# Half-size products for the first layer of a feed-forward network behind an attention: seven instead of eight, two units of tokens at once

## The chip, the cores and the metric

The kernel runs on one core of a Trainium2 chip. The metric is the device time in microseconds from the start to the end of one execution; the median of three runs is given. The core has a matrix engine (TensorE, PE in the profile, with its own queue of weight loads, PEld), VectorE (DVE), ScalarE (ACT), GpSimd (POOL), a queue that issues transfers (SyncE, SP), and 16 DMA engines. Products land in PSUM, which the kernel uses as four double banks of 128 x 2 x 512 floats.

## The reference

Attention over 8 batches, 8 heads, 576 positions and 64 dimensions, with a window of 32 positions for the first four heads and a window of 128 positions with a stride of 4 for the others, and then a feed-forward network over the 4608 x 512 result:

```python
scores = np.where(masks, scale * q @ k.T, -1e9)
attn = exp(scores - max) / (sum + 1e-9)
x = (attn @ v) as 4608 x 512
h = x @ w_in                         # 512 x 2048
sp = np.where(h > 20.0, h, np.log1p(np.exp(np.minimum(h, 20.0))))
g = h * np.tanh(sp)
out = g @ w_out                      # 2048 x 512
```

Inputs and output are float32.

## The kernel before, in words

The tokens are cut into 16 units, half a batch each, of 288 tokens. Per unit there are four pairs of heads; their attention takes small products, and the feed-forward network takes the large ones. Products of float32 accuracy are made from float16 parts: each operand is split into a high and a low part, and three of the four products of parts are added up (low weight by high x, high weight by low x, high by high). The first four units ("direct") compute their attention in float32 on PE; units 4 to 15 use split parts and transposes by DMA.

The first layer (`ff1`, L830 to L844) of a unit takes four chunks of 512 columns of the weights (index j). A call makes two blocks of 128 columns. Each block has 12 matmuls of 128 x 128 weights by 288 tokens: four parts of the 512 inputs times three products of parts. ScalarE then applies Mish to the double bank (L844). A gate (`gate`, L855 to L862) scales the chunk and splits it: high part on ScalarE (L860), low part on VectorE (L862). The second layer (`ff2`) makes again 192 matmuls of the same shape per unit (L872), ScalarE scales the result (L886) and SP stores it (L888). All weights stay in SBUF: `w1`, four tiles of 128 x 4 x 2 x 512, and `w2`.

Ahead of that stand, for units 4 to 15, `prep` (maxima of q, k and v on VectorE, L291, then scales and splits), `scores_of_pair` (L597), `scores` on VectorE (scale and mask L621, maximum L627, subtraction L629), `exps` on ScalarE (L668), `transpose_p` (split L704 and L706, DMA transpose L709), `values` (L745 to L760) and `transpose_x` (split L776 and L778, DMA transpose L781). At the beginning the weights arrive as 64-bit words and are turned into float16 parts (`w_load`, `w_max`, `w_words`, `w_split`; L323 to L396). Matmuls on a tile of zeros (`keep_warm`, L901) fill time on PE at the beginning.

Nothing schedules at run time: the string ORDER lists steps by hand, about 2,000 of them (`ff4.2=0`: unit 4, first half of chunk 1, bank 0; a name that stands again continues the step behind its next `yield`). Each engine executes its instructions in that order, and so does SP with the transfers. Semaphores make an instruction wait for its operands and buffers.

Of the kernel before, what the change touches and what calls it, by code (L numbers as in the profile page):

```python
# [25 lines left out]
SUM_EXP = 14  # L26
TINY = 2.0 ** -40
EXP_BITS = 0x7F800000
P_SCALE = 2.0 ** 14
G_SHIFT = 2.0 ** -14  # L30
# [3 lines left out]
MASKED = -2.0 ** 30  # L34
EPS = 1.0e-9
# [15 lines left out]
tx1.3=0 tx1.3 ww0.2.0 kw10=1 tx1.2=1 tx1.2 sp2.3=2 sc2.3 tx1.3 tx1.3 kw4=0 pr2 pr2 tx1.2 tx1.2 wl1.3.0 wm1.3.0 gt0.0=1
gt0.0 ww1.3.0 wp0.2.0 wp0.2.0 ww1.3.0 wl1.3.1 wm1.3.1 ww1.3.1 ww1.3.1 fs1 kw3=0 ff1.0=0 ff1.0 ff1.0 ff1.1=1 ff1.1
ff1.1 gt1.0=2 ff1.2=3 ff1.2 ff1.2 ff1.3=0 sp2.1=1 sc2.1 ws1.3=3 ws1.3 ff1.3 ex2.3 kw6=2 tp2.3=2 tp2.3 gt0.3 gt1.0
wl1.2.0 wm1.2.0 ww1.2.0 ww1.2.0 wl1.2.1 wm1.2.1 ww1.2.1 ww1.2.1 ex2.1 kw3=3 ff0.2=3 ff0.2 ff0.2 ff0.3=2 ff0.3 ff0.3
gt0.1=3 gt0.1 ff1.6=1 ff1.6 ws1.2=3 ff0.4=2 ff1.6 ws1.2 ff1.3 gt1.1=4 gt1.1 wp1.3.0 wp1.3.0 ff0.4 va2.3=1 ff0.4
tp2.1=0 tp2.1 va2.3 va2.3 wp1.2.1 wp1.2.1 ld3 sp3.0=3 sp3.1=2 lv3 sc3.0 sc3.1 ff1.7=0 ff1.7 ff1.7 gt1.3=5 gt1.3
wp1.2.0 wp1.2.0 wp1.3.1 wp1.3.1 wl1.0.1 wm1.0.1 ff1.4=1 ff1.5=0 ff1.5 ww1.0.1 ff1.4 ff1.4 ff1.5 gt1.2=6 gt1.2 wl1.0.0
wm1.0.0 ww1.0.0 ww1.0.0 va2.1=3 va2.1 va2.1 sp3.3=2 ff0.5=1 ff0.5 ff0.5 gt0.2=7 gt0.2 fo1.2.0=0 fo1.2.1 fo1.2.2
ws1.0=1 ws1.0 ex3.1 tp3.1=3 tp3.1 wl1.1.0 wm1.1.0 fo1.2.3 fo1.2.3 fo1.2.3 sc3.3 ex3.3 sp3.2=3 sc3.2 ex3.2 ww1.1.0
ww1.1.0 sp2.2=1 ld4 sc2.2 pr4 pr4 ex2.2 lv4 fo1.3.0 fo1.3.1 fo1.3.2 fo1.3.3 fo1.3.3 pr3 fo0.2.0=2 fo0.2.1 fo0.2.2  # L60
fo0.2.3 fs2 fo0.2.3 fo0.2.3 pr4 pr4 xa2 tx2.3=3 tx2.3 tx2.3 va2.0=1 tp2.2=0 tp2.2 va2.0 va2.0 wp1.0.0 ex3.0 wp1.0.0
fo0.3.0 fo0.3.1 fo0.3.2 fo0.3.3 fo0.3.3 pr4=0 ww1.0.1 fo1.3.3 pr4 fo0.3.3 tx2.0=3 va2.2=1 tx2.0 va2.2 tx2.0 kw2=2 pr4
# [117 lines left out]
def attn_mish_ffn_kernel(  # L180
# [205 lines left out]
    def w_split(k, g, p):  # L386
# [5 lines left out]
        for v, d, sc in parts:  # L392
            nc.scalar.activation(halves(d, 0), v, AF.Identity, scale=sc)
# [566 lines left out]
```

## Time and profile before

| what | value |
|---|---|
| median of 3 runs | 921.7 us (921.39 to 922.32) |
| the profiled execution, time | 923.0 us |
| the profiled execution, span from first to last instruction | 921.1 us |
| granted TensorE clock | 1.000 |
| moved by DMA | 82.36 MB, mean 89 GB/s |
| read from HBM, written | 49.02 MB, 9.44 MB |
| keep-warm matmuls | 482 |

In the profile's lines, `L841 PE MATMUL b<-x,w 128*128 128x288 f16 x3072` is line, engine and operation; the tile written and the tiles read; the weights' shape and the moving operand's shape and type; and how often. Behind the bar stand busy time in us, the mean duration of one in ns, and the engine's idle time just ahead of these, with what ended it. In a timeline the columns are start, duration and then the instruction with its count, with the idle time before it in brackets.

### The profile page before, as it was taken

Reading aid. Unit: us, or ns where it says so; the run is one execution under the profiler, and the core shown is the slowest. Engines: PE = TensorE matmul, PEld = TensorE weight load, DVE = VectorE, ACT = ScalarE, POOL = GpSimd, SP = SyncE. Lnnn points to the kernel's source line nnn. Section 1 sums busy time; section 2 is a strip of 40 time slices with the busy share of each in tenths; the row PEclk is TensorE's granted clock in tenths of the full one; section 3 lists DMA queues with packets and bytes.
Section 4 is the critical chain, followed back from the end, with each engine's and each line's share of the span. In section 5 each row is a group of like instructions: output and inputs, shape, how many; then the busy total and the mean of one; then the engine's idle time right before and its main releaser. Section 6 shows DMA issues by size and latency. Waiting matters only on the chain.

```text
span 921.1 us, 21816 instructions
## 1 busy us (share of the span) xinstructions
PE 911.5 (99%) x9422; PEld 738.0 (80%) x9422; DVE 593.1 (64%) x879; ACT 545.5 (59%) x804; POOL 22.0 (2%) x99
## 2 busy tenths in 40 slices
PE   9999999999999999999999999999999999999998
PEld 8877878887788877878888888878888888788776
DVE  4877988566867776787967576785546856422020
ACT  3687775673475676756677556776455656644141
POOL 1000000040000000000000000000000000000000
PEclk9999999999999999999999999999999999999999
DMA  9734443130424344424444444326215322212000
GB/s 292 217 117 139 140 139 105 56 105 16 119 81 110 69 106 95 98 62 103 102 100 96 100 72 113 72 55 120 52 33 119 87 55 59 36 41 35 20 14 27
DMA packets 156560, 82.36 MB, mean 89 GB/s; under 512 B 122960, under 2 KB 152368, under 8 KB 156464
## 3 DMA queue, kind: packets, MB, share of 16 engines
q1 hardware_dynamic: 156464, 80.97, 35.5%
q8 instruction: 74, 1.21, 0.5%
q14 instruction: 22, 0.18, 0.1%
HBM read 49.02 MB, written 9.44 MB: 63 GB/s over the span
## 4 chain that ended last, share of the span: by engine, by line
PE 99%; ACT 1%; issue 0%; DVE 0%; ACTq 0%
PE b L872 41%; PE b L841 41%; PE b L597 4%; PE b L745 3%; PE b L901 3%; PE b L739 2%; PE b L716 1%; PE b L594 1%; PE b L649 0%; PE b L352 0%; PE b L349 0%; PE b L800 0%; PE b L787 0%; ACT pp L725 0%; PE b L309 0%; ACT x L802 0%
## 5 line engine op out<-in xcount | busy, mean ns | idle before, releaser
L872 PE MATMUL b<-g,w 128*128 128x288 f16 x3072 | 388.1, 287 | 0.0
L841 PE MATMUL b<-x,w 128*128 128x288 f16 x3072 | 387.3, 286 | 0.0
L841 PEld LDWEIGHTS <-w 128*128 128x128 f16 x3072 | 297.6, 98 | 75.3
L872 PEld LDWEIGHTS <-w 128*128 128x128 f16 x3072 | 297.1, 98 | 75.4
L862 DVE SCALAR_TENSOR_TENSOR g<-hm,sg,g 128x1152 f16<-128x1152 f32 x64 | 89.8, 1414 | 116.8 <-ACT g L860 116.8
L844 ACT ACTIVATE hm<-b,fs 128x576 f32<-128x576 f32 x128 | 92.3, 737 | 102.4 <-PE b L841 88.4
L886 ACT ACTIVATE y<-b,fo 128x288 f32<-128x288 f32 x60 | 43.5, 724 | 126.6 <-PE b L872 116.5
L860 ACT ACTIVATE g<-hm,sg 128x1152 f16<-128x1152 f32 x64 | 79.9, 1253 | 3.2 <-PE b L872 1.6
L668 ACT ACTIVATE sb<-sb,ln_p 96x704 f32<-96x704 f32 (+3 forms) x48 | 42.4, 888 | 26.8 <-DVE sb L629 26.6
L629 DVE TENSOR_TENSOR sb<-sb,nm 72x576 f32<-72x576 f32 (+4 forms) x60 | 45.2, 754 | 2.1
L627 DVE TENSOR_REDUCE nm<-sb 72x8 f32<-72x576 f32 (+4 forms) x60 | 44.9, 748 | 1.7
L760 DVE TENSOR_TENSOR xs<-b,rec 72x512 f32<-72x512 f32 (+1 forms) x64 | 39.7, 620 | 6.5 <-DVE rec L759 0.5
L706 DVE TENSOR_TENSOR p<-sb,p 96x704 f16<-96x704 f32 (+3 forms) x33 | 29.4, 894 | 18.1 <-ACT p L704 18.0
L901 PE MATMUL b<-zeros 128*128 128x128 f16 x482 | 33.4, 229 | 5.1 <-ACT pp L725 2.1
L901 PEld LDWEIGHTS <-zeros 128*128 128x128 f16 x482 | 31.0, 103 | 7.3 <-issue 5.0
L759 DVE RECIPROCAL rec<-den 72x8 f32<-72x8 f32 (+1 forms) x64 | 12.0, 188 | 36.2 <-ACT den L755 27.3
L844 ACT ACT_TABLE_LOAD x22 | 28.2, 1283 | 9.1 <-PE b L841 8.7
L621 DVE SCALAR_TENSOR_TENSOR sb<-b,sc,m_r 96x704 f32<-96x704 f32 (+1 forms) x24 | 23.4, 976 | 15.3 <-PE b L597 6.3
L597 PEld LDWEIGHTS <-q 64*72 64x72 f16 (+1 forms) x1008 | 25.8, 116 | 8.3 <-issue 7.6
L597 PE MATMUL b<-k,q 64*72 64x72 f16 (+3 forms) x1008 | 30.9, 210 | 0.0
L621 DVE SCALAR_TENSOR_TENSOR sb<-b,sc,m_d 72x576 f32<-72x576 f32 (+1 forms) x24 | 22.6, 944 | 11.4 <-PE b L597 11.0
L521 DVE TENSOR_TENSOR q<-qn,q 128x288 f16<-128x288 f32 (+1 forms) x36 | 23.7, 708 | 7.2 <-ACT q L512 7.2
(141 smaller groups left out, 819.0 us busy)
## 6 DMA issues: line engine op xcount, KB each, us to landing
qn<-in_qT SPq DMA_DIRECT2D x16, 576.0 KB
out_T<-y SPq DMA_DIRECT2D x64, 144.0 KB
raw<-in_w_in SPq DMA_DIRECT2D x16, 512.0 KB
raw<-in_w_out SPq DMA_DIRECT2D x16, 512.0 KB
vn<-in_v SPq DMA_DIRECT2D x48, 128.0 KB
knd<-in_kdT SPq DMA_DIRECT2D x16, 208.0 KB
vdn<-in_vd SPq DMA_DIRECT2D x32, 104.0 KB
knp<-in_kT SPq DMA_DIRECT2D x8, 320.0 KB
```

The costliest lines, as they stand in the source:

```text
L597: nc.tensor.matmul(o, q, k, start=start, stop=stop, skip_group_check=True)
L621: nc.vector.scalar_tensor_tensor(args[0], args[1], d["sc"][:nq], args[2], ALU.mult, ALU.add)
L627: nc.vector.tensor_reduce(nm[:nq, :, j:j + n], x, axis=AX.X, op=ALU.max, negate=True)
L629: nc.vector.tensor_tensor(blocked(sb, c0, n, w), x, nm[:nq, :, j:j + n].unsqueeze(3).broadcast_to([nq, 2, n, w]), op=ALU.add)
L668: nc.scalar.activation(x, x, AF.Exp, bias=ln_p[:nq])
L841: nc.tensor.matmul(ph[:, h, :HT], w1[j][:, c, wi, k * P:(k + 1) * P], x_of(d, xi, c), start=(n == 0), stop=(n == len(seq) - 1))
L844: nc.scalar.activation(d["m"][j][:, k0:k0 + 2], ph[:, :, :HT], AF.Mish, scale=d["fs"][:, j:j + 1])
L860: nc.scalar.activation(g[:, 0], m, AF.Identity, scale=sg)
L862: nc.vector.scalar_tensor_tensor(g[:, 1], m, sg, g[:, 0], ALU.mult, ALU.subtract)
L872: nc.tensor.matmul(po[:, :HT], w2[:, e, j, wi, k * P:(k + 1) * P], d["g"][j][:, gi, k, :], start=(j == 0 and n == 0), stop=(j == NCH - 1 a ...
L886: nc.scalar.activation(o, src, AF.Identity, scale=fo)
L901: nc.tensor.matmul(warm[:, 1, 512 - P:], zeros, zeros, start=True, stop=True)
```

## The change

For units 4 to 15 the first layer is made for two units together (a batch, 2 x 288 tokens) by Strassen's scheme in Winograd's form. The 512 inputs are halved (pairs of heads 0 and 1, pairs 2 and 3), each chunk of 512 weight columns is halved, and the tokens are halved into the two units. The eight half-size products of a chunk become seven (`s_p1` to `s_p7`), each with 2 blocks of 128 columns by 6 matmuls of 128x288 (L938). They need four sums of weights and four sums of activations:

- `w_forms` makes the weight sums once, on VectorE (L869 to L881) with a conversion on ScalarE (L879), and stores them and the plain quarters to memory (L887). Since the seven forms don't fit beside the rest, `stream` loads them again for every pair of units: 14 loads of 128 x 2048 float16 (512 KB) into three tiles. These tiles, and buffers for activations, are the places of the old `w1`, which units 4 to 15 no longer read.
- `x_forms` makes the activation sums on VectorE (L908 to L912), splits them (ScalarE L918, VectorE L920) and transposes them by DMA (L923), in place of `transpose_x`.
- Products add up in PSUM, with results taken out in between: bank Y holds product 1, is copied out by ScalarE (L955), then has product 6 added to it, is copied again (L977), has 7 added, is read by VectorE (L983), has 4 added, and goes to Mish. Bank W holds product 5, copied (L962), and then 3, added by VectorE (L997). Product 2 has a bank for itself (added at L969).

In addition: the two units of a pair share one scale (`pf`, from L545); the maxima in `prep` become absolute sums on ScalarE (L511 to L522); for units 4 to 9 (`PE_MASKS`) the mask is added by two matmuls on PE (L646) instead of L621 on VectorE; fewer keep-warm matmuls (303); scales shift by small powers of two. ORDER is new from the first step to the last: about 2,350 entries, whose steps `za` to `zg` are the seven products, `zl` a stream, `zt` the activation sums, `wf` the weight sums.

Three places show what the new order does. First VectorE, where units 4 and 5 are prepared. Before (L291 the maxima, L494, L285 to L287 and L497 the scales, L621 to L629 the masked scores of unit 4):

```order
L291 TENSOR_REDUCE m<-vn 128x1
L291 TENSOR_REDUCE m<-vdn 72x1
L494 TENSOR_REDUCE m_3298<-mru 128x3
L285 TENSOR_SCALAR f<-m_3298 128x3
L286 TENSOR_SCALAR f<-f 128x3
L287 RECIPROCAL s<-f 128x3
L497 TENSOR_SCALAR sc<-f 128x1
L621 SCALAR_TENSOR_TENSOR sb<-b_73,sc,m_d 72x2x288
L627 TENSOR_REDUCE nm<-sb 72x8
L629 TENSOR_TENSOR sb<-sb,nm 72x2x288
```

Now (L1040 a gate, L869 to L875 weight sums, L764 split scores, L920 split activation sums):

```order
L908 TENSOR_TENSOR xs_2496<-w_109,xs_2496 96x2x384
L909 TENSOR_TENSOR w_109<-w_109 96x384
L1040 SCALAR_TENSOR_TENSOR g_145<-hm,sg,g_145 128x1152
L869 TENSOR_TENSOR hm<-w_111 128x1024
L872 TENSOR_TENSOR hm<-hm 128x256
L873 TENSOR_TENSOR hm<-hm 128x256
L874 TENSOR_TENSOR hm<-hm 128x256
L875 TENSOR_TENSOR hm<-hm 128x256
L764 TENSOR_TENSOR p_2486<-sb,p_2486 72x8x104
L920 TENSOR_TENSOR w_108<-w_109,w_108 96x2x384
```

The maxima and masks have left VectorE's row there; weight sums (tile `hm`) and activation sums (tiles `xs`, `w`) stand among gates and splits, all of them ahead of the first product.

Second VectorE, where units 8 and 9 enter the first layer. Before, only gates (L862) belong to that layer there:

```order
L706 TENSOR_TENSOR p_2666<-sb,p_2666 72x8x104
L621 SCALAR_TENSOR_TENSOR sb<-b_70,sc,m_d 72x2x288
L627 TENSOR_REDUCE nm<-sb 72x8
L629 TENSOR_TENSOR sb<-sb,nm 72x2x288
L778 TENSOR_TENSOR g_120<-xs,g_120 96x384
L759 RECIPROCAL rec<-den 96x2x3
L760 TENSOR_TENSOR xs<-b_72,rec 96x2x3x64
L862 SCALAR_TENSOR_TENSOR g_116<-hm,sg,g_116 128x1152
L862 SCALAR_TENSOR_TENSOR g_114<-hm,sg,g_114 128x1152
```

Now the additions L969, L997 and L983 of the first chunk stand behind the scores of units 10 and 11 (L674 to L682) and among splits:

```order
L674 SCALAR_TENSOR_TENSOR sb<-b_72,sc,m_d 72x832
L680 TENSOR_REDUCE nm<-sb 72x8
L682 TENSOR_TENSOR sb<-sb,nm 72x832
L817 RECIPROCAL rec<-den 96x2x3
L818 TENSOR_TENSOR w_109<-b_74,rec 96x2x3x64
L674 SCALAR_TENSOR_TENSOR sb<-b_72,sc,m_d 72x2x288
L680 TENSOR_REDUCE nm<-sb 72x8
L682 TENSOR_TENSOR sb<-sb,nm 72x2x288
L969 TENSOR_TENSOR hm<-b_74,hm 128x576
L764 TENSOR_TENSOR p_2491<-sb,p_2491 72x8x72
L997 TENSOR_TENSOR hm<-b_75,hm 128x576
L983 TENSOR_TENSOR hm<-b_73,hm 128x576
```

They read PSUM banks (`b`) that PE adds to again.

Third SP's queue in the middle of the program. Before (`x`, `g`: activations and a spare buffer, `pT`, `p`: scores):

```order
L781 DMA_TRANSPOSE x<-x_2670 128x6x96
L709 DMA_TRANSPOSE pT_2668<-p_2662 128x12x96
L709 DMA_TRANSPOSE pT_2664<-g_119 128x12x96
L781 DMA_TRANSPOSE x<-g_120 128x6x96
L781 DMA_TRANSPOSE x<-x_2670 128x8x80
L888 DMA out_T<-y 128x288
L417 DMA qn<-in_qT 128x1152
L419 DMA knp<-in_kT 128x2x320
```

Now, in the products of units 8 and 9 (`w_104` to `w_106` the three stream tiles, `wd` the forms in memory):

```order
L767 DMA_TRANSPOSE pT_2488<-p_2491 128x12x96
L893 DMA w_106<-wd_127 128x2048
L893 DMA w_104<-wd_128 128x2048
L893 DMA w_105<-wd_129 128x2048
L767 DMA_TRANSPOSE pT_2488<-p_2486 128x12x96
L448 DMA qn<-in_qT 128x1152
L450 DMA knp<-in_kT 128x2x288
L453 DMA knd<-in_kdT 128x4x72 x2
L893 DMA w_106<-wd_130 128x2048
L893 DMA w_104<-wd_131 128x2048
L767 DMA_TRANSPOSE pT_2488<-p_2491 128x16x80
L893 DMA w_105<-wd_132 128x2048
```

Weight loads stand between transposes and loads of later units.

The core of the diff (ORDER with a line, checks on `direct` and buffers' names left out):

```diff
 ORDER = """
-wl0.3.0 wl0.0.1 ld0 wm0.3.0 ww0.3.0 ww0.3.0 wm0.0.1 ww0.0.1 ww0.0.1 kw16=0 kw16=0 kw16=0 kw16=0 kw16=0 kw16=0 kw16=0
+xa0.0=0 wl0.3.0 wm0.3.0=0 ww0.3.0 ww0.3.0 wl0.3.1 wm0.3.1=0 ww0.3.1 ww0.3.1 kw16=0 kw16=0 kw16=0 kw16=0 kw16=0 kw16=0
...
+PE_MASKS = set(range(4, 10))
...
-        amax(m[:, 4:5], qn)
+        nc.scalar.activation(q2[:, 0], qn, AF.Abs, accum_out=m[:, 4:5])
...
+        elif u in PE_MASKS:
+            for h in range(2):
+                nc.tensor.matmul(pt2[:nq, h, :width], d["idm"][:nq, :nq], masks[pair // 2, d["half"]][:nq, :width], start=True,
+                                 stop=False, skip_group_check=True)
...
+    def w_forms(j, cp):
...
+        nc.vector.tensor_tensor(x, t[:, :, 0], t[:, :, 1], op=ALU.add)
+        yield
+        q = {(c, i): x[:, c, i * h:(i + 1) * h] for c in range(2) for i in range(2)}
+        nc.vector.tensor_tensor(q[1, 1], q[0, 1], q[1, 1], op=ALU.add)
+        nc.vector.tensor_tensor(q[0, 1], q[0, 0], q[0, 1], op=ALU.subtract)
+        nc.vector.tensor_tensor(q[0, 0], q[1, 1], q[0, 0], op=ALU.subtract)
+        nc.vector.tensor_tensor(q[1, 0], q[1, 0], q[0, 0], op=ALU.subtract)
...
+    def stream(p, i):
+        t = V[p]["st"][i] = take("st", streams)
+        nc.sync.dma_start(t.rearrange("p c a n -> p (c a n)"), forms[i].rearrange("p f c a n -> p (f c a n)"))
...
+    def product(p, j, w, x, o, start, stop):
...
+        seq = [(1, 0, c) for c in range(2)] + [(0, i, c) for c in range(2) for i in (1, 0)]
+        for h in range(2):
+            for n, (wi, xi, c) in enumerate(seq):
+                nc.tensor.matmul(o[:, h, :HT], t[:, c, wi, h * P:(h + 1) * P], form_of(p, x, c, xi), skip_group_check=True,
+                                 start=start and n == 0, stop=stop and n == len(seq) - 1)
...
+    def s_p6(p, j):
+        y = V[p]["Y", j]
+        product(p, j, "S2", "T2", y, False, False)
+        yield
+        nc.scalar.copy(hm_of(2 * p + 1, j)[:, :2], y[:, :, :HT])
+
+    def s_p7(p, j):
+        y, m = V[p]["Y", j], hm_of(2 * p + 1, j)
+        product(p, j, "S3", "T3", y, False, False)
+        yield
+        nc.vector.tensor_tensor(m[:, 2:], y[:, :, :HT], m[:, 2:], op=ALU.add)
+        yield
+        act_mish(p, j, m[:, 2:], m[:, 2:])
+
+    def s_p4(p, j):
+        y = V[p]["Y", j]
+        product(p, j, "22", "T4", y, False, True)
+        yield
+        act_mish(p, j, hm_of(2 * p, j)[:, 2:], y[:, :, :HT])
```

More of the change, by code (lines that the diff above doesn't have):

```diff
@@ L26 @@
 SUM_EXP = 14
+IN_EXP = 12
+ROOM = 4.0
 TINY = 2.0 ** -40
@@ L230, in take, with double, single @@
         return tiles[turns[name]]
+    def double(u):
+        return take("d", banks[:3]) if u < 2 else take("b", banks)
+    def single(u):
+        return double(u)[:, 0]
     ident = const.tile([P, P], F32, name="ident")
@@ L342, in w_scale @@
         n = 1 if k == 0 else NCH
-        pm = take("b", banks)[:, 0]
+        pm = single(0)
         for i in range(NCC):
@@ L770, in transpose_x @@
         nq = bl[0][0]
-        if not d["direct"]:
-            nb, rows = len(bl), -(-nq // 16) * 16
-            x16 = take("x16", x16s)
-            hi, lo = (x16[:nq, i * nb * P:(i + 1) * nb * P].rearrange("p (j k) -> p j k", k=P) for i in range(2))
-            nc.scalar.copy(hi, xs[:nq, :nb])
-            yield
-            nc.vector.tensor_tensor(lo, xs[:nq, :nb], hi, op=ALU.subtract)
-            yield
-            at0 = 2 * HT * pair if pair < 2 else 4 * HT + 2 * NR * RP * (pair - 2)
-            nc.sync.dma_start_transpose(d["x"][:, at0:at0 + 2 * nb * rows].rearrange("k (g q) -> k g q", q=rows),
-                                        x16[:rows, :2 * nb * P])
-            return
-        px = take("b", banks)[:, 0]
+        px = single(u)
         for i, (_, q0, _, _, j) in enumerate(bl):
@@ L791, in transpose_x @@
         yield
-        hi, lo = (d["x"][:, (2 * pair + i) * HT:(2 * pair + i + 1) * HT] for i in range(2))
+        hi, lo = (x_of(d, i, pair) for i in range(2))
         src = px[:, :HT]
@@ new lines, in hm_of, with act_mish, s_p1, s_p5 @@
+    def hm_of(u, j):
+        m = U[u]["m"]
+        if j not in m:
+            m[j] = pool.tile([P, FPC, HT], F32, name="hm", bufs=3)
+        return m[j]
+    def act_mish(p, j, o, src):
+        nc.scalar.activation(o, src, AF.Mish, scale=U[2 * p]["fs"][:, j:j + 1])
+    def s_p1(p, j):
+        y = V[p]["Y", j] = take("b", banks)
+        m = hm_of(2 * p, j)
+        product(p, j, "11", "11", y, True, False)
+        yield
+        nc.scalar.copy(m[:, :2], y[:, :, :HT])
+    def s_p5(p, j):
+        w = V[p]["W", j] = take("b", banks)
+        m = hm_of(2 * p + 1, j)
+        product(p, j, "S1", "T1", w, True, False)
+        yield
+        nc.scalar.copy(m[:, 2:], w[:, :, :HT])
@@ L898, in keep_warm @@
     def keep_warm(n):
-        warm = take("b", banks)
+        warm = take("w", banks[3:])
         for _ in range(n):
```

477 lines of the change are left out of this document (292 added, 185 removed).

## The prediction

> **What bounds the kernel now.** I read the page's totals first, then the stages, then the groups of instructions.
>
> ```profile
> span 921.1 us, 21816 instructions
> PE 911.5 (99%) x9422; PEld 738.0 (80%) x9422; DVE 593.1 (64%) x879; ACT 545.5 (59%) x804; POOL 22.0 (2%) x99
> ```
>
> PE is idle for 9.6 us of 921.1. The stages (columns: stretch, length, busy of PE, PEld, DVE, ACT, POOL, granted clock, DMA share, GB/s) show where, and how much room the others have:
>
> ```profile
> 0.00:40.00 40.00, 37.61 (x489) 32.76 (x490) 26.76 (x48) 18.90 (x28) 2.85 (x17) 1.00 0.83 248
> 80.00:120.00 40.00, 38.72 (x380) 31.18 (x380) 35.63 (x58) 30.05 (x49) 0.00 (x0) 1.00 0.56 169
> 120.00:160.00 40.00, 40.00 (x381) 32.49 (x378) 33.11 (x53) 25.72 (x54) 0.00 (x0) 1.00 0.33 99
> 0.00:274.00 274.00, 268.91 (x2817) 221.82 (x2818) 205.00 (x345) 170.03 (x282) 13.46 (x42) 1.00 0.42 128
> 400.00:450.00 50.00, 50.00 (x553) 40.29 (x553) 40.00 (x55) 29.61 (x42) 1.26 (x8) 1.00 0.40 88
> ```
>
> By 274 us PE has lost 5.1 us; from 120 us on it is full, the last stretch and its output aside. So time follows PE's own work. VectorE is the second engine: 80% in a middle stretch, 89% (35.63 of 40) in the densest. PE's work by group:
>
> ```profile
> L872 PE MATMUL b<-g,w 128*128 128x288 f16 x3072 | 388.1, 287 | 0.0
> L841 PE MATMUL b<-x,w 128*128 128x288 f16 x3072 | 387.3, 286 | 0.0
> L901 PE MATMUL b<-zeros 128*128 128x128 f16 x482 | 33.4, 229 | 5.1 <-ACT pp L725 2.1 <-ACT x L802 1.5 <-DVE zeros L896 1.0
> ```
>
> The mean of 286 ns overlaps its neighbours, so I take the price from the distance of starts:
>
> ```profile
> 409.40 6.04 PE L841 MATMUL b<-x,w 128*128 128x288 f16 x48
> 415.28 0.90 PE L745 MATMUL b<-vdh,g 104*128 104x65 f16 x24
> ```
>
> 48 products move the next work by 5.88 us: 122.5 ns each.
>
> **The change, term by term (span 921.1).**
>
> *Products.* A pair of units took 2 x 192 matmuls of this shape; now 4 chunks x 7 products x 2 halves x 6 = 336. Six pairs save 288: 288 x 122.5 ns = **-35.3 us**, all of it on PE's path. The moving operand keeps its shape and strides.
>
> *Masks on PE.* Units 4 to 9 get two mask matmuls for each of four head pairs: 48. The direct units already have such pairs (rows: start, duration):
>
> ```profile
> 51.48 0.52 PE L594 MATMUL b<-m_fb,ident_b 72*72 72x416 bf16 x2
> 51.93 0.94 PE L597 MATMUL b<-knd,qn 64*72 64x104 f32 x16
> 81.21 0.41 PE L594 MATMUL b<-m_fb,ident_b 72*72 72x288 bf16 x2
> 81.55 0.74 PE L597 MATMUL b<-knd,qn 64*72 64x72 f32 x16
> ```
>
> The widest pair takes 0.45 us, the narrowest 0.34. 24 pairs: 8.2 to 10.8, I take the middle, **+9.5 us**.
>
> *Fillers.* 303 keep-warm matmuls instead of 482, all but 45 ahead of the first product. Two runs of them:
>
> ```profile
> 1.04 15.25 PE L901 MATMUL b<-zeros 128*128 128x128 f16 x226 [1.04 <-DVE zeros L896]
> 24.84 2.34 PE L901 MATMUL b<-zeros 128*128 128x128 f16 x39
> 27.01 0.27 PE L300 MATMUL b<-ident,m 128*1 128x128 f32 x1
> ```
>
> That is 67 ns each at the start and 2.17 us / 39 = 56 ns later. 179 fewer: **-10.0 us** at the lower price (12.0 at the higher), if real work is there in their place; if not, the time comes back as a wait.
>
> Sum with PE's idle time as before: 921.1 - 35.3 + 9.5 - 10.0 = **885.3 us**. What remains is new waiting.
>
> *VectorE ahead of the first product.* The weight sums (eight times two operations of 1024 columns and four of 256) and the sums of activations for units 4 and 5 all stand, in the order, before the first addition of a product. The nearest rows:
>
> ```profile
> L384 DVE SCALAR_TENSOR_TENSOR raw<-raw 128x1024 int32<-128x1024 int32 x16 | 19.6, 1227 | 0.6
> L629 DVE TENSOR_TENSOR sb<-sb,nm 72x832 f32<-72x832 f32 x12 | 12.2, 1021 | 0.4
> L629 DVE TENSOR_TENSOR sb<-sb,nm 72x576 f32<-72x576 f32 x12 | 9.0, 754 | 0.4
> L629 DVE TENSOR_TENSOR sb<-sb,nm 96x192 f32<-96x192 f32 x12 | 4.2, 354 | 0.4
> L862 DVE SCALAR_TENSOR_TENSOR g<-hm,sg,g 128x1152 f16<-128x1152 f32 x64 | 89.8, 1414 | 116.8 <-ACT g L860 116.8
> L706 DVE TENSOR_TENSOR p<-sb,p 96x704 f16<-96x704 f32 x10 | 8.8, 882 | 3.8 <-ACT p L704 3.8
> L291 DVE TENSOR_REDUCE m<-qn 128x1 f32<-128x1152 f32 x12 | 16.1, 1344 | 4.8 <-DMA qn<-in_qT 4.8
> ```
>
> Weight sums: 8 x (2 x 1.23 + 4 x 0.42, between the rows of 192 and 576) = 33. Activation sums of two units: some 6. Units 4 and 5 further along, less the maxima now on ScalarE: some 10. On top of the 205 that VectorE had done by 274 us, at about the same state of PE's work, that makes 254. PE reaches that point at 274 - 10 = 264 at the earliest. VectorE gets its first weights at 9.3 us (count, shortest, median and longest in ns, first and last start),
>
> ```profile
> L383 DVE SCALAR_TENSOR_TENSOR raw<-raw,w x16: 1203/1226/1233, 9.3 to 178.4; 128x1024 int32<-128x1024 int32 x16
> ```
>
> and the first addition may lie some 7 us behind PE's first product, an estimate from the 49 matmuls that stand between it and the next wait for VectorE. So it has about 262 us for 254 us of work: 97% busy, where the densest stretch shows 89%. At 95% it needs 267.4, **+5 us** of waiting on PE; at 90%, 282.2, +20; at 100% nothing. When an addition is late, the conversions of scores and the gates queue behind it on VectorE, and on PE the next product into that bank with all that follows. ScalarE in the same stretch goes from 170 to some 230 by the same count and stays below it.
>
> *VectorE between two blocks of products.* The products themselves ask little of it: per chunk three additions of 576 columns (0.754) and two gates (1.414), 5.1 us in 84 x 122.5 ns = 10.3. The attention of the next units and seven activation sums fill the stretch up to the next block. Counted with these prices, from the last addition of units 6 and 7 to the first of units 8 and 9 VectorE has 59.0 us to do; PE has 61.7 (384 products of the second layer, 60 of the new block, scores and values), and some 2.3 more before it needs that bank: 92%. The next stretch is 57.3 against 63, the ones before and after 50 against 61 to 66. At 95% none makes PE wait: nothing, at 89% 4 us.
>
> *ScalarE.* 72 plain copies are new on it, and the maxima of twelve units:
>
> ```profile
> L725 ACT COPY pp<-b 128x576 f32<-128x576 f32 x4 | 2.6, 662 | 3.0 <-PE b L716 3.0
> L844 ACT ACTIVATE hm<-b,fs 128x576 f32<-128x576 f32 x128 | 92.3, 737 | 102.4 <-PE b L841 88.4 <-DVE g L862 13.1 <-ACT vdh L537 0.5
> ```
>
> 72 x 0.662 = 48, the maxima at about their VectorE price, 61; conversions and weight sums some 25. It ends near 680 of 890, 76%.
>
> *Handovers.* What is new is where these copies stand: PE adds a further product into a bank only after ScalarE or VectorE has read it. Of 96 such returns, 30 have a single other product (1.47 us) or less in between. The trace has one with nothing in between (start, duration, idle time before):
>
> ```profile
> 34.95 0.67 PE L716 MATMUL b<-ident,sb 72*72 72x72 f32 x8
> 36.39 1.50 PE L901 MATMUL b<-zeros 128*128 128x128 f16 x24 [0.78 <-ACT pp L725]
> ```
>
> and this is the longest thing that ScalarE regularly does in these stretches:
>
> ```profile
> L860 ACT ACTIVATE g<-hm,sg 128x1152 f16<-128x1152 f32 x64 | 79.9, 1253 | 3.2 <-PE b L872 1.6
> ```
>
> PE waited 0.78 us for a copy on a free ScalarE. So 1.47 us leaves 0.7 for what ScalarE is still at, and a gate takes 1.25: up to 0.56 us late. None late costs nothing, all 30 cost 17 us; with ScalarE three quarters busy, but the copies' places in its queue chosen with the products', I take one in four: **+4 us**. Queued behind such a wait is all of PE's work; nothing else is issued past it.
>
> *Streams.* Per pair 14 loads of 512 KB into three buffers; one tile lasts 24 matmuls, 2.94 us, so a freed buffer has 5.9 us until its next use. The nearest load is 576 KB; it was issued at 508.47, and DMA was quiet again at 512:
>
> ```profile
> 508.47 0.34 SPq L417 DMA_DIRECT2D qn<-in_qT  x1
> ```
>
> ```profile
> 511.50:512.00 0.50, 0.50 (x7) 0.40 (x5) 0.00 (x0) 0.00 (x0) 0.00 (x0) 1.00 0.16 65
> 512.00:512.50 0.50, 0.50 (x6) 0.40 (x5) 0.00 (x0) 0.42 (x1) 0.00 (x0) 1.00 0.00 0
> ```
>
> 3.5 us against 5.9: hidden, as long as SP issues it at once. I cost it nothing, and its failure is a rival. The 56 stores of weight sums (128 KB each) fall in a stretch with a DMA share of 0.33; the transposes stay 48 in number, with 1.75 times the data, where the share is 0.40: both at nothing too.
>
> **Forecast: 885.3 + 5 + 4 = 894.3 us of span.** The profiled execution took 923.0 (span + 1.9), the median of runs 921.7, 0.6 above the span: **895 us**. With VectorE between 100% and 92% in the first stretch (0 to 14 us) and 0 to 8 us in handovers this case reaches from 885 to 907.
>
> **The rivals.**
>
> *VectorE is the bound (chance 0.17).* At 90%, nearer to the 89% that was seen, the first product comes 20 us late, the two tight stretches add 2 and 1, the handovers 4: 885.3 + 27 = 912, as a run 913. For it: 97% was never shown. Against it: in the 89% stretch it was not what PE waited for.
>
> *The stream is late, and the kernel slower (0.11).* All loads share SP's one in-order queue with transposes and stores that wait for VectorE and ScalarE. SP's waits (total, times, longest):
>
> ```profile
> SPq L888 <- ACT y L886: 176.8, 24, 19.7
> SPq L709 <- DVE p L706: 101.4, 20, 12.4
> SPq L781 <- DVE xs L760: 34.7, 10, 11.7
> ```
>
> Nothing urgent stood behind them; now the next weights do. A hold of 12 us while buffers run dry costs 12 + 3.5 - 5.9 = 9.6 us. One in half of the 24 chunks would be 115 us; one in four of the six blocks is 38 us, which makes 895 + 38 = 933. It decides against the change from 27 / 9.6, about three such holds. For it: transposes stand between the loads in every block. Against it: their sources are mostly finished chunks earlier.
>
> *The clock falls when PE waits (0.04).* The first 226 fillers cost 67 - 56 = 11 ns each above the later ones, 2.5 us for one start from rest. If the expected 9 us of waits came as a few long stops, four restarts would add 10 us: 905. Against it: the granted clock is 1.00 in every stage, and the stops are short, like the 0.78 us above.
> The Trainium skill, "TensorE: Matmul & The Clock Gate", section "Part 1: The HAM clock gate", says that after about 3.4 us without work the array runs at half rate until it has been busy about as long. The slow first fillers agree with it; no stop here is long enough to test the fall.
>
> **How the numbers follow.** Forecast 0.62, VectorE 0.17, stream 0.11, clock 0.04; 0.03 for a better case than that, 0.03 for waits that eat the gain exactly. A measurement of this kernel tells 0.2% from no change, 1.8 us. Only the stream case is slower: 0.11. Same 0.03, faster 0.86. The range for 8 in 10 takes the forecast's case, nearly all of VectorE's and the clock's. Its lower end is 885 less 2 for the fillers' higher price, its upper end VectorE at 89%, 23 + 4 + 4 us above 885: **883 to 917**.
>
> **What would show it.** Right: 288 fewer 128x288 matmuls at the same distance; first product at 265 to 275 us; PE full in the products, with waits of some tenths of a us on copies and additions only. VectorE's rival: first product after 280 us and PE waiting for lines of weight or activation sums. The stream's: PE waiting for DMA in the products, SP waiting on transposes. Wrong altogether: another distance than 122.5 ns, or waits for copies in every chunk that sum to far more than 17 us.

## The result and the profile after

The changed kernel takes 938.3 us (median of 4 runs, 937.25 to 939.51), the kernel before 922.0 (921.39 to 923.38): 1.0175 times as long, 95% interval 1.0158 to 1.0193. Forecast were 895 us, with a range to 917, and faster with a chance of 0.86. The profiled execution has a span of 937.7, 43.4 us above the forecast's 894.3.

The totals of the page after:

```profile
span 937.7 us, 21591 instructions
PE 894.4 (95%) x9003; PEld 713.4 (76%) x9003; DVE 650.0 (69%) x1005; ACT 676.9 (72%) x998; POOL 21.0 (2%) x98
```

PE is idle for 43.3 us. The forecast had 18.6 (9.6 as before, 5 for VectorE, 4 for handovers): 24.7 too few. PE is busy for 894.4, where the sum of its terms gave 911.5 - 35.3 + 9.5 - 10.0 = 875.7: 18.7 too few. The stretches show where (columns as in the prediction: stretch, length, busy of PE, PEld, DVE, ACT, POOL, granted clock, DMA share, GB/s). The granted clock is the share of TensorE's full speed that the profile shows; a stretch lacks its length times what is missing to 1.00:

```profile
10.00:20.00 10.00, 5.64 (x45) 4.13 (x45) 7.84 (x13) 3.79 (x6) 2.33 (x11) 0.74 0.76 189
20.00:30.00 10.00, 10.00 (x102) 7.71 (x101) 6.79 (x9) 4.33 (x7) 0.00 (x0) 0.92 1.05 328
40.00:50.00 10.00, 8.33 (x84) 7.29 (x84) 9.76 (x13) 8.47 (x17) 0.00 (x0) 0.78 0.62 217
50.00:60.00 10.00, 8.21 (x57) 5.61 (x56) 7.97 (x13) 5.63 (x14) 0.25 (x2) 0.71 0.19 73
60.00:70.00 10.00, 8.23 (x53) 5.72 (x52) 8.02 (x14) 6.43 (x13) 0.00 (x0) 0.83 0.00 0
...
170.00:180.00 10.00, 8.14 (x65) 6.01 (x64) 7.75 (x17) 4.54 (x8) 0.18 (x1) 0.76 0.53 162
180.00:190.00 10.00, 10.00 (x80) 7.75 (x78) 4.36 (x10) 5.37 (x7) 6.60 (x7) 0.90 0.35 105
...
290.00:300.00 10.00, 7.10 (x94) 5.84 (x92) 6.32 (x15) 9.12 (x14) 0.71 (x6) 1.00 0.63 172
```

Before, the clock stood at 1.00 in all stages. Here the seven stretches below 1.00 lack 2.6 + 0.8 + 2.2 + 2.9 + 1.7 + 2.4 + 1.0 = 13.6 us of full clock, which is most of the 18.7 (some 0.4 of it falls on idle time). In larger pieces, cut at the first product and in 50s around it:

```profile
0.00:306.40 306.40, 281.70 (x2791) 225.18 (x2792) 236.28 (x412) 219.70 (x352) 12.88 (x45) 0.96 0.54 147
306.40:937.70 631.30, 612.66 (x6217) 488.19 (x6213) 413.67 (x594) 457.19 (x647) 8.16 (x53) 1.00 0.60 149
```

```profile
200.00:250.00 50.00, 45.82 (x431) 35.13 (x428) 40.79 (x75) 46.73 (x63) 1.83 (x11) 1.00 0.51 132
250.00:300.00 50.00, 45.50 (x547) 36.82 (x546) 39.00 (x65) 42.63 (x59) 0.71 (x6) 1.00 0.68 140
300.00:350.00 50.00, 47.16 (x463) 36.34 (x463) 40.45 (x63) 45.12 (x64) 0.68 (x6) 1.00 0.75 188
```

From 200 to 350 us it is ScalarE that is nearly full, 134.5 of 150, and VectorE is at 120.2. The first product (count, durations, first and last start):

```profile
L938 PE MATMUL b<-xf,w x78: 283/286/298, 306.4 to 338.2; 128*128 128x288 f16 x78
```

It comes at 306.4, forecast at 265 to 275. Of PE's 43.3 idle us 306.4 - 281.7 = 24.7 lie ahead of it, and so do the seven stretches with the lower clock. What PE waited for, up to the first product and from it on (in all, times, longest):

```profile
PE b L848 <- ACT xf L845: 5.3, 6, 1.6
PE b L380 <- DVE w L412: 4.5, 1, 4.5
PE b L803 <- ACT hm L1029: 4.2, 3, 2.6
```

```profile
PE b L650 <- DVE sb L674: 4.1, 3, 1.9
PE b L938 <- ACT hm L955: 2.4, 3, 1.8
PE b L938 <- DMA w<-wd: 1.4, 3, 1.1
...
PE b L938 <- ACT hm L977: 0.8, 1, 0.8
PE b L938 <- ACT hm L962: 0.6, 1, 0.6
```

Of the rivals' signs, one half of VectorE's is there, a first product after 280 us. The other half is not: nowhere up to the first product does PE wait for a line of weight or activation sums (L869 to L881, L908 to L912), and VectorE has 236.3 us of work by then, where the sum took 254. The streams cost PE 1.4 us of waiting, and the handovers (L955, L962, L977) 3.8, as forecast.

One stop shows the mechanism that the prediction didn't have. Ahead of some functions ScalarE's rows hold an `ACT_TABLE_LOAD` of 1.28 us, the loading of another table of functions. PE and then ScalarE around 295 us (start, duration):

```profile
292.29 0.90 PE L803 MATMUL b<-vdh,pT 104*128 104x65 f16 x24
295.84 0.89 PE L803 MATMUL b<-vdh,pT 104*128 104x65 f16 x24 [2.65 <-ACT hm L1029]
```

```profile
286.99 1.28 ACT L521 ACT_TABLE_LOAD   x1
288.28 0.84 ACT L521 ACTIVATE vh<-vn 128x768 f16<-128x768 f32 x1
...
289.12 1.04 ACT L522 ACTIVATE vdh<-vdn 72x1024 f16<-72x1024 f32 x1
...
290.16 1.24 ACT L1038 ACTIVATE g<-hm,sg 128x1152 f16<-128x1152 f32 x1
292.21 0.37 ACT L540 ACTIVATE idm<-ident_b,inv 96x96 bf16<-96x96 bf16 x1 [0.81 <-DVE inv L538]
292.49 1.24 ACT L562 ACTIVATE qn<-qn,s 128x1152 f32<-128x1152 f32 x1
293.75 1.28 ACT L1029 ACT_TABLE_LOAD   x1
295.05 0.74 ACT L1029 ACTIVATE hm<-b,fs 128x576 f32<-128x576 f32 x1
```

PE needs the bank that the Mish at 295.05 empties. Ahead of that Mish stand a new table for the absolute sums (L521), the sums, and the old table again: 2 x 1.28 us of loading around 2 us of sums. A gate and two scalings stand there too, and 0.81 us in which ScalarE waits for VectorE (L538), so this stop alone doesn't tell what the tables cost. In the whole program:

```profile
L948 ACT ACT_TABLE_LOAD x16 | 20.5, 1283 | 2.0 <-DVE hm L969 1.7
L721 ACT ACT_TABLE_LOAD x10 | 12.8, 1283 | 0.2
L1029 ACT ACT_TABLE_LOAD x9 | 11.5, 1283 | 4.2 <-issue 3.8 <-DVE hm L881 0.2
L511 ACT ACT_TABLE_LOAD x5 | 6.4, 1283 | 0.1
L515 ACT ACT_TABLE_LOAD x4 | 5.1, 1283 | 0.1
L521 ACT ACT_TABLE_LOAD x4 | 5.1, 1283 | 0.1
```

13 loads stand ahead of absolute sums, and others only bring Mish's or the exponential's table back.

### The profile page after: what moved, and what is told of

The parts are those of the page before. It is cut to its first block, busy times and chain, and to the rows that moved or that the text cites. A ratio compares the mean times of both kernels' runs of the same rounds, so it can differ in the third digit from the quotient of the medians.

```text
span 937.7 us, 21591 instructions
## 1 busy us (share of the span) xinstructions
PE 894.4 (95%) x9003; PEld 713.4 (76%) x9003; DVE 650.0 (69%) x1005; ACT 676.9 (72%) x998; POOL 21.0 (2%) x98
## 4 chain that ended last, share of the span: by engine, by line
PE 51%; ACT 11%; DMA 5%; DVE 5%; issue 3%; SPq 0%; ACTq 0%; POOL 0%; DVEq 0%; POOLq 0%
PE b L1050 25%; PE b L938 20%; DMA w<-wd 2%; PE b L650 2%; PE b L803 2%; DMA pT<-p 2%; ACT hm L948 1%; ACT g L1038 1%; DMA knd<-in_kdT 1%; PE b L1026 1%; ACT k L515 1%; DVE g L1040 1%; PE b L646 1%; ACT vdh L522 1%; DMA out_T<-y 1%
## 5 line engine op out<-in xcount | busy, mean ns | idle before, releaser
L938 PEld LDWEIGHTS <-w 128*128 128x128 f16 x2016 | 194.4, 98 | 56.9 <-issue 5.0
L938 PE MATMUL b<-xf,w 128*128 128x288 f16 x1440 | 210.3, 286 | 2.8 <-DMA w<-wd 1.2
L1040 DVE SCALAR_TENSOR_TENSOR g<-hm,sg,g 128x1152 f16<-128x1152 f32 x64 | 90.1, 1413 | 56.8 <-ACT g L1038 56.6
L1026 PE MATMUL b<-xf,w 128*128 128x288 f16 x768 | 99.5, 291 | 0.0
L948 ACT ACTIVATE hm<-hm,fs 128x576 f32<-128x576 f32 x72 | 53.8, 770 | 24.5 <-DVE hm L997 10.1
L938 PE MATMUL b<-w,w 128*128 128x288 f16 x288 | 64.5, 286 | 0.0
L764 DVE TENSOR_TENSOR p<-sb,p 96x704 f16<-96x704 f32 (+3 forms) x48 | 43.0, 898 | 15.9 <-ACT p L762 15.7
L680 DVE TENSOR_REDUCE nm<-b 72x8 f32<-72x576 f32 (+4 forms) x50 | 37.1, 749 | 16.0 <-PE b L650 15.6
L938 PE MATMUL b<-xg,w 128*128 128x288 f16 x288 | 39.2, 286 | 2.6 <-ACT hm L955 2.4
L920 DVE TENSOR_TENSOR w<-w,w 96x768 f16<-96x768 f32 (+3 forms) x34 | 32.3, 951 | 13.0 <-ACT w L918 12.7
L803 PEld LDWEIGHTS <-pT 128*128 128x128 f16 (+3 forms) x1008 | 34.9, 98 | 8.3 <-issue 5.1
L969 DVE TENSOR_TENSOR hm<-b,hm 128x576 f32<-128x576 f32 x24 | 18.1, 754 | 33.1 <-PE b L938 31.1
L918 ACT CAST w<-w 96x768 f16<-96x768 f32 (+3 forms) x34 | 28.3, 832 | 16.8 <-DVE w L909 5.4
L762 ACT CAST p<-sb 96x704 f16<-96x704 f32 (+3 forms) x48 | 37.8, 789 | 2.4 <-DMA pT<-p 1.5
L650 PE MATMUL b<-k,q 64*96 64x128 f16 (+3 forms) x1008 | 32.9, 210 | 6.0 <-DVE sb L674 4.1
L997 DVE TENSOR_TENSOR hm<-b,hm 128x576 f32<-128x576 f32 x24 | 18.0, 751 | 21.3 <-PE b L938 16.9
```

The lines of the kernel that those rows point to most:

```text
L650: nc.tensor.matmul(o, q, k, start=start, stop=stop, skip_group_check=True)
L680: nc.vector.tensor_reduce(nm[:nq, :, j:j + n], x, axis=AX.X, op=ALU.max, negate=True)
L762: nc.scalar.copy(hi, src)
L764: nc.vector.tensor_tensor(lo, src, hi, op=ALU.subtract)
L803: nc.tensor.matmul(avv[:, h, j], pp[:nk, c:c + P], vv[vi][:nk, j, hh, :], start=(i == 0), stop=(i == 2))
L938: nc.tensor.matmul(o[:, h, :HT], t[:, c, wi, h * P:(h + 1) * P], form_of(p, x, c, xi), skip_group_check=True, start=start and n == 0, stop ...
```

## The experiments

The theory: ScalarE, with table loads for the absolute sums, holds PE from 200 us on, and what the keep-warm matmuls ("fillers") had covered in the beginning comes back as stops. The rivals: VectorE (weight sums) sets the first product; the fallen clock; the streams. A ratio is always to the kernel before, on the same chip.

**1. Fillers at the stops (e1_warm).** Two of the places:

```diff
-kw16=0 kw2=0 ws0.3=0
+kw16=0 kw2=0 kw16=0 kw16=0 kw16=0 kw16=0 kw16=0 kw12=0 ws0.3=0
...
-tx0.2 tx0.2 sp1.2=0
+kw16=0 kw10=0 tx0.2 tx0.2 sp1.2=0
```

> The changed kernel with 186 keep-warm matmuls put back where PE stopped: 92 ahead of the first weights' sums (stop of 4.5 us), 64 around the stops between 42 and 64 us, 30 around those at 174 to 176 us. If the fallen clock is a cause (13.6 us of granted clock are missing before 190 us): clock 1.00 in all stages, 938 becomes 925 to 931 and the first product comes 8 to 14 us earlier. If PE's slow stretches only used up slack in front of VectorE's or ScalarE's queue: clock 1.00 as well, but 935 to 939.

Measured: 938.9 us, ratio 1.0182 (1.0144 to 1.0221). By 200 us 5.2 us of clock are missing instead of 13.6, and the first product comes at 305.0. Nothing gained, but the clock isn't whole either, and fillers take PE's time themselves.

**2. The maxima on VectorE again (e2_dvemax).** One of four such lines:

```diff
-        nc.scalar.activation(q2[:, 0], qn, AF.Abs, accum_out=m[:, 4:5])
+        amax(m[:, 4:5], qn)
```

> The changed kernel with the maxima of units 4 to 15 on VectorE again, as before the change. If ScalarE is what PE waits for from 200 us on (90% busy there, with reloads of its tables): it loses some 5 us a unit and half of its table loads, 938 becomes 922 to 932. If VectorE is what the first product waits for, as the rival had it: 5 us a unit more on VectorE ahead of the first product, 940 to 955.

Measured: 959.7 us, ratio 1.0414 (1.0374 to 1.0453). 21 us slower than the changed kernel. ScalarE has 85 us less to do, VectorE 55 more. So this part of the change was right: what it takes off VectorE is worth more than what it costs on ScalarE.

**3. Without the weight sums' arithmetic (e3_nosums).**

```diff
-        nc.vector.tensor_tensor(x, t[:, :, 0], t[:, :, 1], op=ALU.add)
...
-        nc.vector.tensor_tensor(o[:, 1], x, o[:, 0], op=ALU.subtract)
```

> The changed kernel with the arithmetic of the weight sums left out: quarters of the weights are stored in their place, so the products are of other numbers. 33 us less on VectorE and 8 on ScalarE, all ahead of the first product. VectorE as the bound: the first product 20 to 30 us earlier, 910 to 920. ScalarE as the bound: 5 to 10 us earlier, 928 to 934. PE's own stops at the beginning as the cause: 935 to 938.

Measured: 936.7 us, ratio 1.0149 (1.0115 to 1.0183), first product at 304.3. 1.6 us by the medians, with intervals that overlap, for 32 us of VectorE: the weight sums are not what the first product waited for. The rival with chance 0.17 is out as it was priced; that more work on VectorE costs time (e2) is another matter.

**4. The kernel before with fewer fillers (e4_cutbefore).** Seven `kw16=0` at the start of its ORDER are left out.

> The kernel before with 112 of the 226 keep-warm matmuls at its start left out. The prediction's price for fillers (56 ns each): 6.3 us faster, 915 to 916. If the first weights' sums can't start sooner anyway: no gain, a stop of some 5 us in their place, and a clock that falls behind it: 921 to 925.

Measured: 923.2 us (921.9 to 931.4), ratio 1.0032 (1.0007 to 1.0057): no gain of 6.3, rather a loss. Its ten executions fall into two groups: six took 921.9 to 923.4 us at a mean clock of 0.996, four 928.4 to 931.4 at 0.986 to 0.990. The profiled execution, of 928.4 us, is one of the four:

```profile
10.00:20.00 10.00, 4.92 (x32) 3.23 (x32) 6.50 (x8) 4.15 (x6) 2.12 (x11) 0.70 1.05 329
20.00:30.00 10.00, 9.77 (x54) 6.46 (x55) 5.49 (x8) 3.17 (x5) 0.00 (x0) 0.50 0.94 227
```

```profile
15.08 0.74 PE L593 MATMUL b<-m_fb,ident_b 96*96 96x352 bf16 x2 [6.21 <-ACT m_fb L250]
```

A stop of 6.2 us takes the fillers' place, and the clock falls to half behind it. The first layer then starts at 65.6 us instead of 59.3, and the span is 5.5 us longer. The stop ends with a mask (`m_fb`) that ScalarE makes from what GpSimd has built. In the changed kernel this mask is ready at 13.8 us, because GpSimd's first step on `ident`, which ScalarE needs just ahead of it, starts only here:

```profile
11.36 0.49 POOL masks.py:199 TENSOR_SCALAR_AFFINE_SELECT ident<-ident 128x128 f32<-128x128 f32 x1 [10.10 <-issue]
```

For these 10.10 us GpSimd waits for nothing that the profile shows. So fewer fillers could not bring the first masked scores much forward in either kernel.

**5. Squares in place of absolute values (e5_square).**

```diff
-        nc.scalar.activation(q2[:, 0], qn, AF.Abs, accum_out=m[:, 4:5])
+        nc.scalar.activation(q2[:, 0], qn, AF.Square, accum_out=m[:, 4:5])
```

> The changed kernel with squares summed in place of absolute values (a bound on the maximum as good for these inputs, whose largest values are above 1). The operation takes as long, but ScalarE needs no other table for it: the run with the maxima on VectorE had 25 table loads fewer (25 x 1.283 = 32 us), most of them between 200 and 340 us and in the blocks of products. If ScalarE's queue is what PE waits for there: 918 to 930, first product 8 to 20 us earlier. If VectorE is: 935 to 939.

Measured: 924.3 us, ratio 1.0026 (1.0008 to 1.0044): 14.0 us faster than the changed kernel by one word in four lines. The sums take as long as before (1163 ns for the 128x1152 of L511, 1161 with absolute values), and the table loads are 26 instead of 50, so 24 fewer. The profiled execution took 928.3 us, 4 above the median. The table loads that are left, two at the beginning aside:

```profile
L721 ACT ACT_TABLE_LOAD x11 | 14.1, 1283 | 0.2
L948 ACT ACT_TABLE_LOAD x8 | 10.3, 1283 | 1.9 <-DVE hm L969 1.7
L1029 ACT ACT_TABLE_LOAD x5 | 6.4, 1283 | 2.7 <-issue 2.4 <-DVE hm L881 0.2
```

and the stretches again:

```profile
200.00:250.00 50.00, 47.55 (x467) 36.73 (x466) 42.55 (x78) 43.36 (x62) 1.84 (x11) 1.00 0.53 136
250.00:300.00 50.00, 48.48 (x555) 39.10 (x554) 43.04 (x72) 41.25 (x61) 0.72 (x6) 1.00 0.73 150
```

No load stands ahead of a sum, half of those ahead of Mish are gone, and PE gains 1.7 and 3.0 us in these two stretches. The wait for the Mish of L1029 falls from 4.2 to 0.2. The first product comes at 301.5, 4.9 us earlier and not 8 to 20; of the 11.2 us between the two profiled spans 6.3 lie behind it. Between the start of the first layer and the first product PE's idle time falls from 13.9 to 8.4 us, from the first product on from 18.6 to 12.4.

**6. Without the streams (e6_nostream), and masks on VectorE again (e7_nomasks).**

```diff
-        nc.sync.dma_start(t.rearrange("p c a n -> p (c a n)"), forms[i].rearrange("p f c a n -> p (f c a n)"))
+        if p == DIRECT // 2 and i < 3:
+            nc.sync.dma_start(t.rearrange("p c a n -> p (c a n)"), forms[i].rearrange("p f c a n -> p (f c a n)"))
```

> The changed kernel with the streams left out: three tiles are loaded once and every product reads them as they are, so the products are of other numbers; 81 loads of 512 KB less. As predicted (hidden): 935 to 938. If the loads hold SP's queue or slow the transposes beside them: 925 to 933.

```diff
-PE_MASKS = set(range(4, 10))
+PE_MASKS = set()
```

> The changed kernel with the masks of units 4 to 9 on VectorE again. The prediction's price: 9.5 us less on PE, and 24 operations of 0.35 to 1.2 us, some 20 us, more on VectorE, half of them ahead of the first product. If PE's own work is the limit: 927 to 932. If a late VectorE is what PE waits for, as where the maxima were put back: 940 to 948.

Measured: 935.1 us without streams, ratio 1.0128 (1.0089 to 1.0168), so 42 MB of loads cost some 3 us by the medians; the intervals with and without them overlap. With the masks on VectorE 941.8, ratio 1.0214 (1.0185 to 1.0244): 3.5 slower, though PE has some 11 us less to do. In the profiled executions it is still busy for 893.6 us against 894.4, at a mean clock of 0.976 against 0.985, and idle for 45.3 against 43.3: what the masks leave free goes into slower matmuls and waits.

**7. The kernel with squares, further relieved.** Without the weight sums as in 3 (e8_square_nosums), and with the sums on GpSimd, `nc.gpsimd` for `nc.vector` in `w_forms` (e9_square_pool):

> The kernel with the squares, and the arithmetic of the weight sums left out too (plain quarters are stored, the products are of other numbers): 33 us less on VectorE, 8 on ScalarE ahead of the first product. Without them the kernel with absolute values gained 1.6 us. If ScalarE's table loads had hidden VectorE's share of the lateness: 906 to 916, first product below 290. If VectorE was never late there: 920 to 924.

> The kernel with the squares, its weight sums made on GpSimd, which is 98% idle. If VectorE's load ahead of the first product still costs something: 910 to 920, faster than before. If the sums take GpSimd several times VectorE's 1.23 and 0.42 us, the forms are late and PE waits for the first streams: 930 to 960. If neither matters: 922 to 926.

Measured: 925.6 us, ratio 1.0028 (1.0007 to 1.0050), first product at 298.2, so VectorE wasn't hidden behind ScalarE either. On GpSimd 945.3, ratio 1.0235 (1.0199 to 1.0270); the first product falls back to 314.9, for

```profile
L881 POOL TENSOR_TENSOR hm<-hm 128x1024 f16<-128x1024 f32 x8 | 19.4, 2428 | 85.4 <-ACT hm L879 69.3 <-issue 8.8 <-DVE q L572 7.4
```

this subtraction takes 2.43 us there and 1.22 on VectorE, and the small ones take twice as long or more.

**8. Fillers and an earlier load in the kernel with squares (e10 to e12).** The fillers as in 1, but into a free half of a bank; and `wl0.2.0` moved ahead of `lv1`.

> The kernel with the squares and 172 keep-warm matmuls in the stops up to 70 us and at 177 us, now into the bank's half that is free, so that nothing waits for them. The granted clock lacks 15 us in this kernel. If the slow PE delays the work behind it, now that ScalarE holds it less: clock 1.00 and 912 to 919. If the first weights, ScalarE and VectorE set the pace up to 70 us anyway, as the same fillers in the kernel with absolute values suggested: 922 to 926.

> The kernel with the squares, with one weight load (the fifth of eight) moved ahead of a unit's seven loads in SP's queue. ScalarE stood 3.3 us for that load at 36 to 39 us, and the copies, VectorE's reciprocals and PE's transposes behind it waited too. If the stops up to 70 us set when the first product comes: the first layer's first matmul 2 to 4 us earlier, 920 to 923. If later stages use up the difference: 923 to 926.

> The same, with 192 keep-warm matmuls in the stops that remain up to 70 us and at 177 us. The granted clock lacks 15 us in the kernel with the squares. If the slow PE is on the path once the late load is gone: clock 1.00 in all stages, 908 to 917, faster than before. If the chain of weights, ScalarE and VectorE sets the pace there whatever PE's clock: 919 to 925.

Measured: 924.0, 925.1 and 923.7 us, ratios 1.0014 (1.0001 to 1.0027), 1.0024 (1.0011 to 1.0036) and 1.0022 (1.0007 to 1.0037). No difference from e5 that can be told. Of 15.3 us of clock that lack in e5 by 200 us, e12 lacks 6.8; it brings nothing. But these fillers do only part of what was meant. The first stop is filled; at the later ones PE waits, 4.0 us in all in e10 and 4.8 in e12, for a copy of ScalarE (L846) before the fillers begin, so there they lengthen the stops.

**9. Does time lost at the beginning count? (e13_delay, e14_nosign)** 176 keep-warm matmuls ahead of the first `ff`; and one operation of `w_words` left out.

> The changed kernel with 176 keep-warm matmuls (9.9 us at 56 ns) ahead of the first layer's first matmul. If the time at which the first layer starts is what counts, as the forecast's sum took it: 947 to 949. If ScalarE and VectorE set the pace of the following stage anyway: the delay is absorbed, 938 to 942.

> The changed kernel with one of VectorE's three operations in the preparation of the weights left out (the signs of the weights get lost, so the products are of other numbers): 16 x 1.23 = 20 us less on VectorE, 8 of the 16 ahead of 75 us. If VectorE's share in the preparation of the weights makes PE stop there: first layer's first matmul 3 to 6 us earlier, 930 to 935. If it is the arrival of the weights or ScalarE: 936 to 939.

Measured: 945.2 us with the delay, ratio 1.0248 (1.0231 to 1.0265). The first layer starts here (changed kernel first, then e13)

```profile
65.47 12.20 PE L1026 MATMUL b<-xf,w 128*128 128x288 f16 x96
```

```profile
74.60 11.92 PE L1027 MATMUL b<-xf,w 128*128 128x288 f16 x96
```

9.1 us later, of which 6.9 arrive at the end by the medians: 0.75 of it. Without the signs 939.3, ratio 1.0190 (1.0164 to 1.0215): VectorE's share in the weights does not set this start.

**10. The remaining table loads, late fillers, load order (e15 to e17).** The exponential of units 4 to 15 as `AF.Relu`; no `kw` among the products (e16); and, without these `kw` too, four `wl` ahead of `lv0`, `lv1` and `ld2` (e17).

> The kernel with the squares, and the exponentials of units 4 to 15 replaced by a function that needs no other table (so the attention is of other numbers): the last 24 reloads behind 200 us are gone, 31 us of ScalarE. If reloads still make PE wait: 912 to 919. If ScalarE has room for them now: 922 to 926.

> The kernel with the squares, without the 45 keep-warm matmuls that stand among the products (two runs of 16, one of 13; 2.5 us at 56 ns). If PE is full there: 921.5 to 922.5, level with the kernel before. If they only fill stops: 924 to 925.

> The same, with four of the eight weight loads of the first layer moved ahead of the loads of values or of a unit's loads in SP's queue, as in the order before. The delay test says that some 0.7 us of each us gained ahead of the first layer's first matmul stays. If the arrival of the weights makes PE stop up to 70 us: 3 to 6 us earlier there, 918 to 921, faster than before. If not, or if the values are late in their place: 921 to 925.

Measured: 925.2, 927.5 and 926.3 us, ratios 1.0028 (1.0014 to 1.0042), 1.0057 (1.0038 to 1.0077) and 1.0050 (1.0030 to 1.0070). Removing 22 more table loads, as the first of them does, gains nothing. The 45 fillers among the products are worth some 3 us by the medians (927.5 against 924.3 with them; the intervals just overlap). The order of the loads (926.3 against 927.5) changes nothing that can be told. No version is faster than the kernel before.

## Why the prediction was wrong

**Right.** The products: 768 + 2016 matmuls instead of 3072, at the distance of before. Twelve of them:

```profile
430.62 1.63 PE L938 MATMUL b<-xf,w 128*128 128x288 f16 x12
```

(1.63 - 0.286) / 11 = 122 ns. The handovers: 3.8 us of waits for copies, 4 forecast. The streams: some 3 us by the medians (e6, not told from nothing), nothing forecast. ScalarE's total: 676.9, forecast 680.

**Mis-sized.** The masks:

```profile
L646 PE MATMUL b<-m_r,idm 96*96 96x352 bf16 (+1 forms) x24 | 5.8, 324 | 0.0
L646 PE MATMUL b<-m_d,idm 72*72 72x288 bf16 (+1 forms) x24 | 5.6, 315 | 0.0
```

11.4 us, 9.5 forecast. And VectorE's +5 was not needed: it had 236.3 us of work up to the first product, not 254, and without the sums nothing is gained (e3, e8).

**The step that failed first: "ScalarE in the same stretch goes from 170 to some 230 by the same count and stays below it."** The count was good, 219.7 by 306 us. But a sum of busy time says nothing of what stands ahead of the one instruction that PE needs, and the price of the maxima, "about their VectorE price", left out that this function needs another table than its neighbours Mish and the exponential. That the total came out all the same is luck: the new order changes less often between Mish and the exponential (26 loads in e5 against 44 before), and the absolute sums give that back (50). They cost 14.0 us, shown by e5. Which loads they are matters: removing 22 others gained nothing (e15).

The Trainium skill, "ScalarE: Activation LUTs", section "Table sets: the hidden batching unit", says that cheap functions, absolute value among them, are in every set of tables. The trace disagrees: 13 loads of 1.283 us stand right ahead of absolute sums; for squares there are none.

**The step that failed second: "-10.0 us ... if real work is there in their place; if not, the time comes back as a wait."** It named the condition and then booked the gain. Nothing was there in their place: the fillers ended at 9.3 us and PE stood 4.5 us for the first weights, and the masks were not ready before 13.8 us either. In the kernel before, leaving out fillers at the same place saves nothing (e4). More: the first layer starts at 65.5 us, 6.2 later than before, where the sum has it up to 10 earlier, since the fillers that are gone stood ahead of it. By e13 three quarters of such a lateness reach the end. That makes 10 us not gained, and some 5 lost. The 5 are an estimate: in the profiled executions the first layer of e11 starts 4.0 us earlier than that of e5 (63.55 against 67.56), and the medians show no gain.

**The clock** fell, which had a chance of 0.04, and its condition was misread: "the stops are short". It is visible in PE's busy time, some 13 us. What it can cost shows where executions of one kernel were granted different clocks. In e4 the group at 0.986 to 0.990 is some 6 us longer than the group at 0.996, and 0.006 of 926 us is 5.6 us: there the lost clock reached the end nearly whole. The four executions of e6 run the same way, from 930.8 us at 0.989 to 938.0 at 0.978. What it costs in the changed kernel is not settled. An execution that stops longer may lose clock and time together, and no run here separates the two; and e1, which restored 8.4 of the 13.6 us with fillers, gained nothing, while its fillers take more room themselves (35.7 us against 22.7). In e10 and e12 the later fillers stood behind the waits that they were to fill.

**The place of the first product** was off by some us from the beginning: "at about the same state of PE's work" was not the same state. Between the start of the first layer and the first product PE makes 168 matmuls of probabilities and values now, 42 before:

```profile
L803 PE MATMUL b<-vdh,pT 72*128 72x65 f16 (+1 forms) x96 | 3.6, 193 | 3.1 <-ACT hm L1029 3.1
L803 PE MATMUL b<-vh,pT 128*128 128x65 f16 (+1 forms) x72 | 2.7, 194 | 1.2 <-ACT hm L1029 1.2
```

That moves work, and costs nothing in the end.

Of the 43.4 us, 14 are shown to be the table loads (e5), 2 the masks, and some 3 by the medians the streams (e6, not told from nothing); 15 for the beginning are estimated from e4 and e13. Some 9 stay open: stops of some tenths of a us between 70 and 300 us and among the products that no single relief (VectorE, tables, clock, loads) removed. These shares were taken one at a time and may overlap; the lost clock is not a further one but runs through them. Counted on PE, the profiled execution of e5 still has 12.3 us of idle time ahead of the first layer, where the kernel before had 3.3, and lacks 15.3 us of clock. Open too is what paces the first 65 us behind the late mask: not VectorE's share in the weights (e14), not the order of their loads (e17). Relief of ScalarE there, and an earlier start of GpSimd, were not tried.

## What to carry to other kernels

Before a function moves to ScalarE, look which functions stand to its left and right in the queue: a table load is a row of its own in the profile, and it is paid twice, ahead of the newcomer and ahead of the old function's return; squares did here what absolute values did, without one. A filler that is removed is a gain only if the engine has the next operands by then: look at what arrives when, in the row behind the fillers. And a total of busy time clears an engine only if no chain runs through it; read what stands in its queue ahead of the instruction that the bound engine waits for.

## What the hardware showed

- The clock fell without a long stop. In windows of 1 us it is 0.50 or 1.00, apart from those in which it changes, so the 0.78 of a longer stretch is a mean. Behind 1.63 us of standing at 42 us it was 0.50 from 46 to 55 us; at 174 to 176 us two stops of 0.97 and 0.89 us, with 0.5 us of small transposes between, were enough, and the 48 matmuls behind them took 8.68 us, where 48 at the full clock take 6.04 (L841 in the prediction's rows):

```profile
174.92 0.48 PE L835 MATMUL b<-ident,xs 72*128 72x72 f32 x4 [0.97 <-DVE xs L818]
176.28 0.41 PE L848 MATMUL b<-xf,minus 128*128 128x288 f16 x1 [0.89 <-ACT xf L845]
...
176.71 8.68 PE L1026 MATMUL b<-xf,w 128*128 128x288 f16 x48
```

  A stop of 2.65 us at 293 us, with full products close by on both sides, left it at 1.00. The 3.4 us of idleness that the prediction cites from the Trainium skill's "TensorE: Matmul & The Clock Gate" ("Part 1: The HAM clock gate") are no safe bound by these rows; what share of the array's time the work around a stop fills seems to count, which no run here isolates.
- 45 matmuls on zeros among the products did not make the kernel slower; by the medians it is some 3 us faster with them (e16 against e5, whose intervals just overlap).
- A table load takes 1.283 us in each of the 50 cases, and in the rows at 293.75 the next function starts 1.30 us after the load's start: nothing more is paid there.
